# A GEGLU kernel's first weight chunk: its second pair of blocks by seven products in place of plain matmuls

## The chip, the cores and the metric

The kernel runs on one core of one Trainium2 chip. The metric is the device time of one execution in microseconds (us). One run of each kernel is profiled.

## The reference

```python
def reference(x, w_gate, w_up, w_down):      # x 1 x 2048 x 1024, w_gate and w_up 1024 x 3584, w_down 3584 x 1024, bf16
    return (_gelu(x @ w_gate) * (x @ w_up)) @ w_down
```

## The kernel before

The kernel takes the tokens in two halves of 1024 (h), each as two token blocks of 512 (tb). It takes the 3584 columns of the weights in chunks of 512, each of two **pairs** of 128-column blocks. A **plain unit** is one column block against one token block: 8 matmuls for gate, 8 for up, then a gelu on ScalarE and a multiply on VectorE. A pair against both token blocks is four plain units, 64 matmuls. Nearly every pair is instead done in the manner of Strassen and Winograd, as a 2 x 2 block product with **seven products** in place of eight: 56 matmuls. For that it needs sums of weight blocks (S1 to S4, per pair, mostly on GpSimd) and sums of blocks of x (T1 to T4, once per half, on VectorE), and M1 to M7 are combined in the PSUM banks by copies (ScalarE) and additions (VectorE). M1 and M2 use unsummed bf16 blocks; the other five use f32 sums (with f32 copies of one block each in M3 and M4).

Only the first chunk of the first half is plain, in all its eight units, because the sums are not there yet. All instructions of an engine run in program order; `dve`, `act`, `pool`, `pe` and `sp` fix that order.

```python
    for kd in range(KH, KD):
        load_xT(xT, 0, 0, kd, kd + 1)
        if kd == KH + 1:
            for j in range(2):
                load_w(first, j, 5, KD, act, 0, FA)
    for j in range(2):
        load_w(first, j, 0, KD, sp, FA, FG)
    for k0 in range(0, KD, KH):
        load_xT(xT, 0, 1, k0, k0 + KH)
    new_chunk((0, 1))
    for j in range(2):
        load_w((0, 1), j, 0, KD)

    # [cut: half()]

    def t_sum(name):
        def b(j, l):
            return xT[l][:, half(j), :]

        t0 = ("t1", "t2", "t3", "b22", "t4").index(name) * KH * TB
        t = t_mem[:, t0 : t0 + KH * TB].rearrange("p (a b) -> p a b", b=TB)
        tsum[name] = t
        sub = ALU.subtract
        tt = nc.vector.tensor_tensor
        if name == "t1":
            dve(tt(out=t, in0=b(0, 1), in1=b(0, 0), op=sub))
        elif name == "t2":
            t1 = tsum["t1"].bitcast(F32)
            dve(tt(out=t, in0=b(1, 1), in1=t1, op=sub))
        elif name == "t3":
            dve(tt(out=t, in0=b(1, 1), in1=b(0, 1), op=sub))
        elif name == "t4":
            t2 = tsum["t2"].bitcast(F32)
            dve(tt(out=t, in0=b(1, 0), in1=t2, op=sub))
        else:
            for c in range(KH):
                act(nc.scalar.copy(out=t[:, c, :], in_=b(1, 1)[:, c, :]))

    # [cut: gelu() is one ScalarE activation, mult() one VectorE multiply into hT, unit_out() both]

    def unit(hT, bset, fi, tb):
        for b, w_sb in zip(bset, chunks[first]):
            for kd in range(KD):
                mm_gu(banks[b], w_sb, fi, tb, kd)
        unit_out(hT, bset, fi, tb)

    # [cut: transpose_x0(), which transposes half of block 0 on TensorE]

    def first_units(hT):

        wg, wu = chunks[first]
        held = (VB, RB)
        transpose_x0(0)
        for kd, j in [(kd, j) for kd in range(KD) for j in range(2)]:
            for u in range(2):
                mm_gu(banks[held[u][j]], (wg, wu)[j], u, 0, kd)
            if (j, kd) == (1, 0):

                transpose_x0(1)
        for u in range(2):
            unit_out(hT, held[u], u, 0)

    # [cut: s_sum(h, pair, j, name): with a(i, kh) the weights of f-block i and contraction half kh,
    #  s1 = a(1,0) + a(1,1), s2 = s1 - a(0,0), s3 = a(0,0) - a(1,0), s4 = a(0,1) - s2; on GpSimd,
    #  or on VectorE if on_dve; a22 is a ScalarE copy of a(1,1)]
    # [cut: pair_quads() up to here; its mm() is the four matmuls of one half of a product, done() runs
    #  what is hung on a point, prep() makes the next pair's sums, add_m5() adds M5 on VectorE]

        def m2():
            for j in range(2):
                mm(P_[j], j, block(key, j, 0, 1), b21, False)
                if j == 0:
                    g[0] = gelu(banks[P_[0]], nxt is None)
                else:
                    mult(hT, g[0], banks[P_[1]], f0, 0)

        def do_m5(j):
            mm(V_[j], j, s(j, "s1"), tsum["t1"], True)
            m5[j] = m_pool.tile([P, TB], F32, name=f"m5_{j}")
            act(nc.scalar.copy(out=m5[j][:], in_=banks[V_[j]][:]))
            prep(j, "s1")

        def do_m6(j):
            mm(QB[j], j, s(j, "s2"), tsum["t2"], False)
            act(nc.scalar.copy(out=banks[RB[j]][:], in_=banks[QB[j]][:]))

        for j in range(2):
            mm(P_[j], j, block(key, j, 0, 0), b11, True)
            act(nc.scalar.copy(out=banks[QB[j]][:], in_=banks[P_[j]][:]))
        behind = len(pending) > 0
        if behind:

            pending.pop()()
        done("m2 of last")
        if behind:
            if nxt is None:
                m2()
                done("m2")
            else:
                pending.append(m2)
            order = (do_m6, 0), (do_m6, 1), (do_m5, 0), (do_m5, 1)
        else:
            pending.append(m2)
            order = (do_m5, 0), (do_m6, 0), (do_m6, 1), (do_m5, 1)
        for f, j in order:
            f(j)
            if (f, j) == (do_m6, 1):
                done("m6")
        for j in range(2):
            add_m5(QB[j], QB[j])
            prep(j, "s2")
        done("m5")
        for j in range(2):
            mm(RB[j], j, s(j, "s3"), tsum["t3"], False)
            add_m5(V_[j], RB[j])
            prep(j, "s3")
            if j == 0:
                g[1] = gelu(banks[V_[0]], nxt is None)
            else:
                mult(hT, g[1], banks[V_[1]], f0 + 1, 1)
        done("m7")
        for j in range(2):
            mm(QB[j], j, s(j, "s4"), tsum["b22"], False)
            prep(j, "s4")
            if j == 0:
                g[2] = gelu(banks[QB[0]], nxt is None)
            else:
                mult(hT, g[2], banks[QB[1]], f0, 1)
        done("m3")
        for j in range(2):
            mm(RB[j], j, s(j, "a22"), tsum["t4"], False)
            prep(j, "a22")
            if j == 0:
                g[3] = gelu(banks[RB[0]], nxt is None)
            else:
                mult(hT, g[3], banks[RB[1]], f0 + 1, 0)

    # [cut: the down projection]

        if h == 0:
            first_units(hT)
            unit(hT, PB, 2, 0)
            t_sum("t1")
            unit(hT, QB, 3, 0)
            t_sum("t2")
            t_sum("b22")
            unit(hT, VB, 0, 1)
            t_sum("t3")
            for name in S_NAMES:
                for j in range(2):
                    s_sum(0, PPG, j, name)
            unit(hT, RB, 1, 1)
            t_sum("t4")
            unit(hT, QB, 2, 1)
            unit(hT, VB, 3, 1)
            first_pair = PPG
```

Of the kernel before, what the change touches and what calls it, by code (L numbers as in the profile page):

```python
# [34 lines left out]
def kernel(  # L35
# [171 lines left out]
    for kd in range(KH, KD):  # L207
        load_xT(xT, 0, 0, kd, kd + 1)
        if kd == KH + 1:
            for j in range(2):  # L210
                load_w(first, j, 5, KD, act, 0, FA)
    for j in range(2):
        load_w(first, j, 0, KD, sp, FA, FG)
    for k0 in range(0, KD, KH):
        load_xT(xT, 0, 1, k0, k0 + KH)
    new_chunk((0, 1))
    for j in range(2):
        load_w((0, 1), j, 0, KD)
# [4 lines left out]
    def half(j):  # L223
        return slice(j * KH, (j + 1) * KH)

    def t_sum(name):
        def b(j, l):
            return xT[l][:, half(j), :]

        t0 = ("t1", "t2", "t3", "b22", "t4").index(name) * KH * TB  # L230
        t = t_mem[:, t0 : t0 + KH * TB].rearrange("p (a b) -> p a b", b=TB)
        tsum[name] = t
        sub = ALU.subtract
        tt = nc.vector.tensor_tensor
        if name == "t1":
            dve(tt(out=t, in0=b(0, 1), in1=b(0, 0), op=sub))
        elif name == "t2":
            t1 = tsum["t1"].bitcast(F32)
            dve(tt(out=t, in0=b(1, 1), in1=t1, op=sub))
        elif name == "t3":  # L240
            dve(tt(out=t, in0=b(1, 1), in1=b(0, 1), op=sub))
        elif name == "t4":
            t2 = tsum["t2"].bitcast(F32)
            dve(tt(out=t, in0=b(1, 0), in1=t2, op=sub))
        else:
            for c in range(KH):
                act(nc.scalar.copy(out=t[:, c, :], in_=b(1, 1)[:, c, :]))


    def mm_gu(ps, w_sb, fi, tb, kd):  # L250
# [33 lines left out]
    def unit_out(hT, bset, fi, tb):  # L284
        mult(hT, gelu(banks[bset[0]]), banks[bset[1]], fi, tb)

    def unit(hT, bset, fi, tb):
        for b, w_sb in zip(bset, chunks[first]):
            for kd in range(KD):
                mm_gu(banks[b], w_sb, fi, tb, kd)  # L290
        unit_out(hT, bset, fi, tb)

    def transpose_x0(q):

        parts = [(2 * q, 0, 4), (2 * q + 1, 0, 4)]
# [15 lines left out]
            else:  # L311
                act(nc.scalar.copy(out=xT[0][:, kd, cols], in_=tp[:, cols]))  # L312

    def first_units(hT):

        wg, wu = chunks[first]
        held = (VB, RB)
        transpose_x0(0)
        for kd, j in [(kd, j) for kd in range(KD) for j in range(2)]:
            for u in range(2):  # L320
                mm_gu(banks[held[u][j]], (wg, wu)[j], u, 0, kd)
            if (j, kd) == (1, 0):

                transpose_x0(1)
        for u in range(2):
            unit_out(hT, held[u], u, 0)


    ssum = {}
# [4 lines left out]
        w_sb = chunks[(key[0], key[2] // PPG)][j]  # L334
        return w_sb[:, half(kh), fi * P : (fi + 1) * P]

    def s_sum(h, pair, j, name, on_dve=False):
        key = (h, "p", pair)

        def a(i, kh):  # L340
            return block(key, j, i, kh)

        if on_dve and name in ("s1", "s2", "s3"):

            if j == 0:
                first_s[name] = wd_pool.tile([P, WDT, D], BF16, name="wd_sb")
            t = first_s[name][:, j, :].bitcast(F32R)
        else:
            s0 = (2 * S_NAMES.index(name) + j) * KH * P
            t = s_mem[:, s0 : s0 + KH * P]  # L350
        t = t.rearrange("p (a b) -> p a b", b=P)
        ssum[(h, pair, j, name)] = t

        def tt(in0, in1, op):
            if on_dve:
                dve(nc.vector.tensor_tensor(out=t, in0=in0, in1=in1, op=op))
            else:
                pool(nc.gpsimd.tensor_tensor(out=t, in0=in0, in1=in1, op=op))  # L358

        if name == "s1":  # L360
            tt(a(1, 0), a(1, 1), ALU.add)
        elif name == "s2":
            s1 = ssum[(h, pair, j, "s1")].bitcast(F32)
            tt(s1, a(0, 0), ALU.subtract)
        elif name == "s3":
            tt(a(0, 0), a(1, 0), ALU.subtract)
        elif name == "s4":
            s2 = ssum[(h, pair, j, "s2")].bitcast(F32)
            tt(a(0, 1), s2, ALU.subtract)
        else:  # L370
            act(nc.scalar.copy(out=t, in_=a(1, 1)))  # L371
# [6 lines left out]
    def pair_quads(hT, h, pair, nxt, then):  # L378
# [67 lines left out]
        if behind:  # L446
# [3 lines left out]
            else:  # L450
                pending.append(m2)
            order = (do_m6, 0), (do_m6, 1), (do_m5, 0), (do_m5, 1)
        else:
            pending.append(m2)
            order = (do_m5, 0), (do_m6, 0), (do_m6, 1), (do_m5, 1)
# [349 lines left out]
    for h in range(NH):  # L805
        hT = hT_pool.tile([P, KF, SH], BF16, name="hT")
        first_pair = 0
        if h == 0:
            first_units(hT)
            unit(hT, PB, 2, 0)  # L810
            t_sum("t1")
            unit(hT, QB, 3, 0)
            t_sum("t2")
            t_sum("b22")
            unit(hT, VB, 0, 1)
            t_sum("t3")
            for name in S_NAMES:
                for j in range(2):
                    s_sum(0, PPG, j, name)
            unit(hT, RB, 1, 1)  # L820
            t_sum("t4")
            unit(hT, QB, 2, 1)
            unit(hT, VB, 3, 1)
            first_pair = PPG
            xs = [(tb, kd) for tb in (1, 0) for kd in range(KD)]
            new_x(1)
            stage_load(0)
# [1 line left out]
        for pair in range(first_pair, NPAIR):  # L829
            then = {}  # L830
            if pair % PPG == 0 and (pair // PPG + 1) * PPG < NPAIR:
# [6 lines left out]

                if key not in chunks:
                    then["m2 of last"] = [load_chunk]  # L840
            if h == 0:

                n = [min(4 * (pair - first_pair + d), NSTEP) for d in range(3)]
                steps = [lambda k=k: stage_step(k) for k in range(n[0], n[1])]
                new = range((n[1] + 2) // 3, (n[2] + 2) // 3)

# [130 lines left out]
```

## Time and profile before

| | before |
|---|---|
| median of 4 runs | 541.58 us (541.51 to 543.56) |
| span of the profiled run | 539.7 us |
| TensorE busy | 535.1 us, 99% |
| VectorE's first multiply (block 0 of the first pair done) | 13.26 us |
| first product of the first seven-product pair | 33.80 us |
| last matmul's record ends, last ScalarE copy starts | 536.32, 536.41 us |

The engines' timelines: the columns are start, length, engine, line, operation, output and input, count, and in brackets how long the engine was idle before and what released it.

```profile
13.26 1.28 DVE L276 TENSOR_TENSOR hT<-w_mem,bank 128x512 bf16<-128x512 f32 x2 [6.30 <-PE bank L252]
...
33.80 1.89 PE L386 MATMUL bank<-xT,w_mem 128*128 128x512 bf16 x8
...
531.63 4.69 PE L656 MATMUL bank<-t_mem,s_mem 128*128 128x512 f32 x20
...
536.41 0.59 ACT L709 CAST o_sb<-bank 128x512 bf16<-128x512 f32 x1 [5.76 <-PE bank L656]
```

From the first multiply (13.26) to the third pair's first matmul (33.80) is the **stretch** that the change rewrites: 20.54 us. From the end of the last matmul to the start of the last ScalarE copy is the **tail**: 536.41 - 536.32 = 0.09 us.

### The profile page before, as it was taken

What the parts mean: (1) busy time and instruction counts of PE and PEld (TensorE: products, weight loads), DVE (VectorE), ACT (ScalarE), POOL (GpSimd) and SP (SyncE); (2) the same over time, 40 slices, a digit from 0 to 9 for tenths busy, and PEclk for the clock granted to TensorE, in tenths of its full rate; (3) what the DMA queues carried; (4) which work ended last, traced back from release to release, by engine and by line L of the source; (5) the groups of instructions that cost most, each with busy time, mean ns of one, the idle gap of its engine ahead of it and who ended that gap; (6) DMA issues with size and microseconds to landing.
All of it is one profiled execution on the core that took longest, in us unless ns stands there. A gap on an engine that the chain in (4) does not pass through costs nothing.

```text
span 539.7 us, 7102 instructions
## 1 busy us (share of the span) xinstructions
PE 535.1 (99%) x2392; PEld 374.5 (69%) x2392; DVE 354.9 (66%) x466; ACT 258.9 (48%) x438; POOL 235.0 (44%) x206
## 2 busy tenths in 40 slices
PE   9999999999999999999999999999999999999997
PEld 3457777666776676767776677777777766866865
DVE  1767777787775997889574434444444469969951
ACT  2435555555555319216465555555555551452270
POOL 0197777777776000000056776666777730000000
PEclk9999999999999999999999999999999999999999
DMA  9928577696827876779950405041331466677946
GB/s 233 310 82 230 185 242 237 184 286 195 277 76 252 299 244 227 249 265 313 327 182 1 155 2 156 7 149 57 99 106 51 157 204 213 226 241 246 291 145 207
DMA packets 84771, 102.70 MB, mean 190 GB/s; under 512 B 18688, under 2 KB 66304, under 8 KB 84736
## 3 DMA queue, kind: packets, MB, share of 16 engines
q1 hardware_dynamic: 61936, 80.30, 46.2%
q10 hardware_dynamic: 22800, 21.96, 13.2%
q8 instruction: 19, 0.31, 0.2%
q14 instruction: 16, 0.13, 0.1%
HBM read 85.98 MB, written 12.58 MB: 183 GB/s over the span
## 4 chain that ended last, share of the span: by engine, by line
PE 98%; DMA 1%; ACTq 0%; ACT 0%; issue 0%
PE bank L386 61%; PE bank L656 33%; PE bank L252 5%; DMA w_mem<-in_w_gate_dram 1%; ACTq L161 0%; ACT xT L312 0%; ACT o_sb L709 0%; ACTq L167 0%; ACTq L709 0%
## 5 line engine op out<-in xcount | busy, mean ns | idle before, releaser
L386 PE MATMUL bank<-t_mem,s_mem 128*128 128x512 f32 x1016 | 239.8, 394 | 0.0
L386 PEld LDWEIGHTS bank<-t_mem,s_mem 128*128 128x128 f32 x1016 | 190.8, 188 | 41.9
L358 POOL TENSOR_TENSOR s_mem<-w_mem 128x512 fp32r<-128x512 bf16 x100 | 115.8, 1178 | 201.3 <-DMA w_mem<-in_w_up_dram 104.6
L276 DVE TENSOR_TENSOR hT<-w_mem,bank 128x512 bf16<-128x512 f32 x104 | 71.3, 686 | 92.4 <-PE bank L386 46.3
L656 PE MATMUL bank<-t_mem,s_mem 128*128 128x512 f32 x544 | 127.2, 392 | 0.0
L656 PEld LDWEIGHTS bank<-t_mem,s_mem 128*128 128x128 f32 x544 | 102.1, 188 | 22.2 <-issue 0.2
L409 DVE TENSOR_TENSOR bank<-bank,m 128x512 f32<-128x512 f32 x104 | 67.3, 694 | 46.9 <-ACT m L431 45.3
L386 PE MATMUL bank<-xT,w_mem 128*128 128x512 bf16 x416 | 94.3, 380 | 0.0
L271 ACT ACTIVATE w_mem<-bank 128x512 f32<-128x512 f32 x104 | 61.9, 596 | 57.7 <-DVE bank L409 32.7
L386 PEld LDWEIGHTS <-w_mem 128*128 128x128 bf16 x416 | 38.7, 98 | 49.7 <-issue 6.5
L566 DVE TENSOR_TENSOR t_mem<-w_mem 128x1024 fp32r<-128x1024 bf16 x56 | 65.5, 1216 | 0.0
L358 POOL TENSOR_TENSOR s_mem<-w_mem,s_mem 128x512 fp32r<-128x512 bf16 x50 | 62.1, 1267 | 0.0
L358 POOL TENSOR_TENSOR s_mem<-s_mem,w_mem 128x512 fp32r<-128x512 f32 x50 | 59.6, 1212 | 0.0
L371 ACT CAST s_mem<-w_mem 128x512 fp32r<-128x512 bf16 x52 | 32.0, 616 | 33.1 <-PE bank L386 29.1
L436 ACT COPY bank<-bank 128x512 f32<-128x512 f32 x52 | 29.6, 570 | 38.1 <-PE bank L386 38.1
L631 DVE TENSOR_TENSOR s_mem<-hT 128x512 fp32r<-128x512 bf16 x52 | 34.2, 685 | 10.2 <-PE bank L656 9.5
L656 PEld LDWEIGHTS <-hT 128*128 128x128 bf16 x224 | 21.3, 98 | 26.6 <-issue 2.1
L431 ACT COPY m<-bank 128x512 f32<-128x512 f32 x52 | 30.5, 587 | 17.1 <-PE bank L386 17.1
L440 ACT COPY bank<-bank 128x512 f32<-128x512 f32 x52 | 29.6, 570 | 13.5 <-PE bank L386 13.5
L709 ACT CAST o_sb<-bank 128x512 bf16<-128x512 f32 x28 | 15.4, 585 | 39.6 <-PE bank L656 39.6
L591 DVE TENSOR_TENSOR o_sb<-wd_sb,o_sb 128x512 fp32r<-128x512 bf16 x28 | 29.4, 1051 | 0.5
L252 PE MATMUL bank<-xT,w_mem 128*128 128x512 bf16 x128 | 28.4, 379 | 0.3 <-DVE xT L310 0.2
(42 smaller groups left out, 250.4 us busy)
## 6 DMA issues: line engine op xcount, KB each, us to landing
t_mem<-t_dram SPq DMA_DIRECT2D x56, 512.0 KB, 5.3
w_mem<-in_w_gate_dram ACTq DMA_DIRECT2D x10, 1024.0 KB, 5.6
w_mem<-in_w_up_dram ACTq DMA_DIRECT2D x10, 1024.0 KB, 9.1
wd_sb<-in_w_down_dram SPq DMA_DIRECT2D x28, 256.0 KB, 5.0
t_dram<-o_sb SPq DMA_DIRECT2D x28, 256.0 KB, 2.4
wd_sb<-in_w_down_dram SPq DMA_DIRECT2D x12, 512.0 KB, 8.8
w_mem<-in_w_down_dram SPq DMA_DIRECT2D x10, 512.0 KB, 6.1
w_mem<-in_w_down_dram SPq DMA_DIRECT2D x4, 1024.0 KB, 6.3
```

Of the source, the lines that this page charges most:

```text
L252: nc.tensor.matmul(ps[:], lhsT=w_sb[:, kd, fi * P : (fi + 1) * P], rhs=xT[tb][:, kd, :], start=(kd == 0), stop=(kd == KD - 1),)
L271: act(nc.scalar.activation(out=g_sb, in_=ps[:], func=ACT.Gelu_apprx_tanh))
L276: nc.vector.tensor_tensor(out=hT[:, fc, tb * TB : (tb + 1) * TB], in0=g_sb, in1=ps[:], op=ALU.mult,)
L358: pool(nc.gpsimd.tensor_tensor(out=t, in0=in0, in1=in1, op=op))
L371: act(nc.scalar.copy(out=t, in_=a(1, 1)))
L386: nc.tensor.matmul(banks[bank][:], lhsT=lhs[:, c, :], rhs=rhs[:, c, :], start=start and c == 0, stop=c == KH - 1, skip_group_check=True,)
L409: nc.vector.tensor_tensor(out=banks[dst][:], in0=banks[src][:], in1=m5[j][:], op=ALU.add)
L431: act(nc.scalar.copy(out=m5[j][:], in_=banks[V_[j]][:]))
L436: act(nc.scalar.copy(out=banks[RB[j]][:], in_=banks[QB[j]][:]))
L566: dve(nc.vector.tensor_tensor(out=t, in0=in0, in1=in1, op=ALU.subtract))
L631: dve(nc.vector.tensor_tensor(out=t, in0=in0, in1=in1, op=op))
L656: nc.tensor.matmul(banks[bset[u]][:], lhsT=lhs(i, u), rhs=rhs(i), start=start and i == 0, stop=stop and i == NS - 1, skip_group_check=True,)
```

## The change

The first chunk's second pair is done by seven products as well. For this its sums must be ready some 14 us earlier than the first sums were before. So both token blocks of the first pair are done first, the transposes of x for block 1 go ahead of the second pair's weights in SyncE's queue (as 2 + 2 + 4 blocks instead of 4 + 4), T3 follows T1 and T2 at once on VectorE, S3 moves from GpSimd to VectorE, and M2, which needs no sums, stands right behind M1 to give the sums time.

```diff
@@ loads at the start
+    for k0, k1 in ((0, 2), (2, KH), (KH, KD)):
+        load_xT(xT, 0, 1, k0, k1)
     for j in range(2):
         load_w(first, j, 0, KD, sp, FA, FG)
-    for k0 in range(0, KD, KH):
-        load_xT(xT, 0, 1, k0, k0 + KH)
     new_chunk((0, 1))
... (t_sum takes a range of contraction blocks, so far always the whole one; unit() goes; part() runs the
    matmuls of units 0 and 1, or of one of them, over a range of contraction blocks)
-    def first_units(hT):
... (the same four held banks for units 0 and 1 of token block 0)
+    def first_pair_units(hT):
+        held = (VB, RB)
+        transpose_x0(0)
+        part(held, 0, 0, 1)
+        transpose_x0(1)
+        part(held, 0, 1, KD)
         for u in range(2):
             unit_out(hT, held[u], u, 0)
+        held = (QB, PB)
+        part(held, 1, 0, KH)
+        t_sum("t1")
+        t_sum("t2")
+        t_sum("b22")
+        t_sum("t3")
+        for u in range(2):
+            part(held, 1, KH, KD, (u,))
+            unit_out(hT, held[u], u, 1)
+        for j in range(2):
+            s_sum(0, 1, j, "s3", True, False)
+        for name in ("s1", "s2", "s4"):
+            for j in range(2):
+                s_sum(0, 1, j, name)
@@ pair_quads
             else:
                 pending.append(m2)
             order = (do_m6, 0), (do_m6, 1), (do_m5, 0), (do_m5, 1)
+        elif "m2" in then:
+            m2()
+            done("m2")
+            order = (do_m5, 0), (do_m5, 1), (do_m6, 0), (do_m6, 1)
         else:
@@ main loop
         if h == 0:
-            first_units(hT)
-            unit(hT, PB, 2, 0)
-            t_sum("t1")
... (the other units and sums of the first chunk)
-            first_pair = PPG
+            first_pair_units(hT)
+            first_pair = 1
...
-            if h == 0:
+            if h == 0 and pair < PPG:
+                then = {
+                    "m2": [lambda j=j: s_sum(0, pair, j, "a22") for j in range(2)]
+                    + [lambda: t_sum("t4")],
+                }
+            if h == 0 and pair >= PPG:
... (the staging of the down weights counts from pair PPG as before)
```

More of the change, by code (lines that the diff above doesn't have):

```diff
@@ L224, in half, with t_sum @@
         return slice(j * KH, (j + 1) * KH)
-    def t_sum(name):
+    def t_sum(name, c0=0, c1=KH):
         def b(j, l):
-            return xT[l][:, half(j), :]
+            return xT[l][:, j * KH + c0 : j * KH + c1, :]
         t0 = ("t1", "t2", "t3", "b22", "t4").index(name) * KH * TB
@@ L232, in t_sum @@
         tsum[name] = t
-        sub = ALU.subtract
-        tt = nc.vector.tensor_tensor
-        if name == "t1":
-            dve(tt(out=t, in0=b(0, 1), in1=b(0, 0), op=sub))
-        elif name == "t2":
-            t1 = tsum["t1"].bitcast(F32)
-            dve(tt(out=t, in0=b(1, 1), in1=t1, op=sub))
-        elif name == "t3":
-            dve(tt(out=t, in0=b(1, 1), in1=b(0, 1), op=sub))
-        elif name == "t4":
-            t2 = tsum["t2"].bitcast(F32)
-            dve(tt(out=t, in0=b(1, 0), in1=t2, op=sub))
-        else:
-            for c in range(KH):
-                act(nc.scalar.copy(out=t[:, c, :], in_=b(1, 1)[:, c, :]))
+        t = t[:, c0:c1, :]
+        if name == "b22":
+            for c in range(c1 - c0):
+                act(nc.scalar.copy(out=t[:, c, :], in_=b(1, 1)[:, c, :]))
+            return
+        in0, in1 = {
+            "t1": lambda: (b(0, 1), b(0, 0)),
+            "t2": lambda: (b(1, 1), tsum["t1"].bitcast(F32)[:, c0:c1, :]),
+            "t3": lambda: (b(1, 1), b(0, 1)),
+            "t4": lambda: (b(1, 0), tsum["t2"].bitcast(F32)[:, c0:c1, :]),
+        }[name]()
+        dve(nc.vector.tensor_tensor(out=t, in0=in0, in1=in1, op=ALU.subtract))
     def mm_gu(ps, w_sb, fi, tb, kd):
@@ L285, in unit_out @@
         mult(hT, gelu(banks[bset[0]]), banks[bset[1]], fi, tb)
-    def unit(hT, bset, fi, tb):
-        for b, w_sb in zip(bset, chunks[first]):
-            for kd in range(KD):
-                mm_gu(banks[b], w_sb, fi, tb, kd)
-        unit_out(hT, bset, fi, tb)
     def transpose_x0(q):
@@ L312, in transpose_x0, with part @@
                 act(nc.scalar.copy(out=xT[0][:, kd, cols], in_=tp[:, cols]))
-    def first_units(hT):
-        wg, wu = chunks[first]
+    def part(held, tb, k0, k1, us=(0, 1)):
+        for kd in range(k0, k1):
+            for j in range(2):
+                for u in us:
+                    mm_gu(banks[held[u][j]], chunks[first][j], u, tb, kd)
+    def first_pair_units(hT):
         held = (VB, RB)
         transpose_x0(0)
-        for kd, j in [(kd, j) for kd in range(KD) for j in range(2)]:
-            for u in range(2):
-                mm_gu(banks[held[u][j]], (wg, wu)[j], u, 0, kd)
-            if (j, kd) == (1, 0):
-                transpose_x0(1)
+        part(held, 0, 0, 1)
+        transpose_x0(1)
+        part(held, 0, 1, KD)
         for u in range(2):
             unit_out(hT, held[u], u, 0)
+        held = (QB, PB)
[10 more added lines that the diff above has]
+        for name in ("s1", "s2", "s4"):
+            for j in range(2):
+                s_sum(0, 1, j, name)
     ssum = {}
@@ L335, in block, with s_sum @@
         return w_sb[:, half(kh), fi * P : (fi + 1) * P]
-    def s_sum(h, pair, j, name, on_dve=False):
+    def s_sum(h, pair, j, name, on_dve=False, staged=True):
         key = (h, "p", pair)
@@ L341, in a @@
             return block(key, j, i, kh)
-        if on_dve and name in ("s1", "s2", "s3"):
+        if on_dve and staged and name in ("s1", "s2", "s3"):
             if j == 0:
@@ L808 @@
         if h == 0:
-            first_units(hT)
-            unit(hT, PB, 2, 0)
-            t_sum("t1")
-            unit(hT, QB, 3, 0)
-            t_sum("t2")
-            t_sum("b22")
-            unit(hT, VB, 0, 1)
-            t_sum("t3")
-            for name in S_NAMES:
-                for j in range(2):
-                    s_sum(0, PPG, j, name)
-            unit(hT, RB, 1, 1)
-            t_sum("t4")
-            unit(hT, QB, 2, 1)
-            unit(hT, VB, 3, 1)
-            first_pair = PPG
+            first_pair_units(hT)
+            first_pair = 1
             xs = [(tb, kd) for tb in (1, 0) for kd in range(KD)]
@@ L840 @@
                     then["m2 of last"] = [load_chunk]
-            if h == 0:
-                n = [min(4 * (pair - first_pair + d), NSTEP) for d in range(3)]
+            if h == 0 and pair < PPG:
[4 more added lines that the diff above has]
+            if h == 0 and pair >= PPG:
+                n = [min(4 * (pair - PPG + d), NSTEP) for d in range(3)]
                 steps = [lambda k=k: stage_step(k) for k in range(n[0], n[1])]
```

## The prediction

> **What bounds the kernel now.** I read the page's busy row first, then its chain that ended last, then the chain in order of time.
>
> ```profile
> PE 535.1 (99%) x2392; PEld 374.5 (69%) x2392; DVE 354.9 (66%) x466; ACT 258.9 (48%) x438; POOL 235.0 (44%) x206
> ...
> PE 98%; DMA 1%; ACTq 0%; ACT 0%; issue 0%
> ```
>
> ```profile
> 8.61 25.34 PE bank L252 x116
> 33.96 150.70 PE bank L386 x672
> 184.66 87.89 PE bank L656 x392
> ```
>
> The reader is to see that TensorE is the path from 8.6 us to the end, without a gap, and that no other engine is above 66%. L252 is the plain first chunk that this change attacks; L386 are the pairs done by seven products; L656 is the down projection, untouched. So only two things can move the time: fewer matmuls in the first chunk, and new gaps of TensorE there.
>
> The rates. ScalarE's timeline shows one gelu per plain unit of 16 bf16 matmuls, and the first copy (L440) of each seven-product pair:
>
> ```profile
> 15.00 0.60 ACT L271 ACTIVATE w_mem<-bank 128x512 f32<-128x512 f32 x1 [1.29 <-PE bank L252]
> ...
> 32.27 0.60 ACT L271 ACTIVATE w_mem<-bank 128x512 f32<-128x512 f32 x1 [2.86 <-PE bank L252]
> ```
>
> Between these two gelus lie five units: 17.27 / 5 = 3.454 us each, 215.9 ns per matmul. The 12 pairs of the second chain line take 150.70 / 12 = 12.56 us for 56 matmuls; 16 of them are bf16 (3.45 us), so the 40 in f32 take 9.10 us, 227.6 ns each. 128 plain matmuls at 215.9 ns are 27.63 us, and 5.24 us (first matmul in TensorE's timeline) plus that plus some 1 us of transposes gives the 33.8 us at which the first product starts: the first chunk has no hidden stall to win back.
>
> **What the Trainium skill says.** "TensorE: Matmul & The Clock Gate", section "Back-to-back issue gap", gives N / 2.4 + 2.5 ns when warm, 215.8 ns for N = 512; the trace has 215.9. "SBUF — State Buffer", section "Who interferes with whom", says that a VectorE instruction with two SBUF inputs contends with a GpSimd instruction that reads SBUF, and that the shared port is an exclusive lock. The trace agrees to a tenth of a microsecond (VectorE's and GpSimd's timelines):
>
> ```profile
> 24.31 2.28 DVE L241 TENSOR_TENSOR t_mem<-xT 128x2048 fp32r<-128x2048 bf16 x1
> 27.76 3.10 DVE L244 TENSOR_TENSOR t_mem<-xT,t_mem 128x2048 fp32r<-128x2048 bf16 x1
> ```
>
> ```profile
> 25.83 1.78 POOL L358 TENSOR_TENSOR s_mem<-w_mem 128x512 fp32r<-128x512 bf16 x1 [1.68 <-DMA w_mem<-in_w_up_dram]
> 27.57 4.32 POOL L358 TENSOR_TENSOR s_mem<-s_mem,w_mem 128x512 fp32r<-128x512 f32 x2
> ```
>
> GpSimd's sum at 25.83 finds the port held by T3 until about 26.45 and ends 1.16 us after that; T4 at 27.76 waits for GpSimd's operation of 27.57 to let go after some 1.0 us, runs its 2.28 us to 30.86, and GpSimd's next one ends 1.0 us later. Each waiter gets the port as the holder leaves; they alternate. "DMA: Bandwidth & Descriptors", section "Queues, rings and completion order", says that on each DMA engine a queue's descriptors are consumed in ring order; so what is issued first on SyncE's queue mostly lands first, which is the reason for moving the transposes of x.
>
> **The change part by part.**
>
> *Removed and added on TensorE.* Before, the four f-blocks of the first chunk are plain: 128 matmuls. After, blocks 0 and 1 are plain on both token blocks (64), and blocks 2 and 3 form a pair (56). One plain pair, 64 x 215.9 = 13.82 us, becomes 12.56 us: **1.26 us** less on the path that sets the end, 541.53 to 540.27 us if nothing waits. That is 0.23%, the whole possible gain.
>
> *The x transposes.* They now stand ahead of the two 512 KB weight loads in SyncE's queue. Before, those weights landed at 12.6 and 14.4 us, the two transposes at 16.4 and 18.3 us (issue plus time to landing in the DMA view). The same bytes in the new order end at the same 18.3 us, so I estimate the 2+2+4 blocks in at about 11.4, 12.5 and 14.6 us and the weights at about 16.5 (gate) and 18.3 (up). TensorE finishes token block 0 at 13.05 us, wants the second block's first transposes then, those of blocks 2-3 at 14.8, the rest at 16.5, and the second pair's weights (M1) at 13.05 + 32 x 0.2159 = 19.96 and 20.8. Each has one to three microseconds of room.
>
> *The sums.* They are the same kinds of work, but now due 14 us earlier. VectorE's order is fixed (the instruction order of both kernels shows it): two multiplies, T1, T2, T3, the multiplies of units 0 and 1, S3 twice, the multiply behind M2, T4, then the additions of M5. GpSimd has S1, S2, S4, two each. From the rows above: T 2.28 us, S on GpSimd 1.15, S on VectorE 0.68, multiply 0.69.
>
> - VectorE's multiplies end at 14.4; T1 to 16.6, T2 to 18.8. GpSimd, waiting since the gate weights landed, takes the port for 1.0 us; T3 runs 19.65 to 21.9.
> - Unit 0's multiply, done by gelu time at 19.1, is behind T3: 21.85 to 22.5. It frees the bank into which M1's second result is copied: copy to 23.15. M2's second half could start at 22.55 and starts at 23.2: **0.65 us lost**.
> - M5, M6, M7 then run without waiting: S1 is ready at 19.8 and 23.0 against 24.1 and 25.0; S2 at 24.1 and 25.65 against 25.9 and 26.8; S3 at 24.6 and 26.2 against 27.7.
> - S3, T4 and GpSimd's S2 and S4 alternate on the port, so T4 runs from 27.06 and ends at 29.3. The addition of M5 into M3's bank stands behind it and ends at 29.95. M3 could start at 23.2 + 0.86 + 24 x 0.2276 = 29.5, starts at 30.0: **0.5 us lost**.
> - Afterwards the third pair starts at 33.65 us against 33.8: its sums (GpSimd, from 29.2 on, eight of 1.15 us) are done before their products.
>
> Sum: -1.26 + 0.65 + 0.5 = -0.1 us: 541.4 us. This is the walk that I consider likeliest.
>
> **The rivals.**
>
> *A: one more GpSimd operation ahead of T3.* If the gate weights land before T2 starts (16.5), GpSimd takes the port both before T2 and before T3, and everything behind T3 moves by 1.0 us: 542.4 us. For it: my landing estimate is 16.5, on the edge. Against: more separate transposes make the queue later rather than earlier.
>
> *C: the port hardly bites.* If the gate weights land after T3 has started (18.8 or later), or VectorE keeps the port between back-to-back sums, the first loss falls to 0.0 to 0.2 us and the second to about 0.3 to 0.5: 540.3 to 540.9. For it: S3 and T3 were placed early on purpose, which looks tuned for this; and two-microsecond gaps were seen between issue and first bytes (the 1 MB load issued at 16.08 has its bytes only from 18.3). Against: the alternation in the lines above.
>
> *D: a transfer becomes the wait.* If the weights of the second pair land after 20 us, M1 waits for DMA, with up to 1 us. Against: the bytes ahead of them are the same as those that were in by 18.3 us before.
>
> *E: the gain appears in full or more* because VectorE or GpSimd work leaves the path elsewhere. Against: TensorE has no gap later, so nothing else can shorten.
>
> **Range and chances.** A 0.2 x 542.4, the walk 0.4 x 541.4, C 0.4 x 540.5 make 541.2 us. D belongs to the tail. The range runs from near the full saving, 540.4, to one port turn lost, 542.4. The three times of before spread from 541.51 to 543.56, so a single late run can hide the sign. Two per cent are 10.8 us; the moved stretch is 14 us long, and nothing in it can grow or shrink by that: same 0.98.
>
> **What would show it right or wrong.** The chain should read L249 x some 58 and then the products; M1 of the second pair should start near 20.0 us with no DMA wait before it. On VectorE, T3 should take 3.2 us (1.0 of them for the port) rather than 2.28; ScalarE's second copy behind M1 should wait for VectorE's multiply; the product bank's matmuls should show gaps of 0.65 us before M2's second half and of 0.5 before M3, with VectorE as releaser. Third pair's M1 at 33.6 us; from there the trace is a copy of the old one. It is wrong if T1, T2 and T3 take 2.28 us each while GpSimd works, if TensorE waits for xT of block 1, or if the third pair itself stalls on GpSimd's S sums, which start later than they did before.

## The result

The changed kernel's median was **541.85 us** (541.73 to 541.90, 4 runs), that of before 541.58. The ratio was 0.9994 with a 95% interval of 0.9976 to 1.0012: the same. The ratio is taken over the fast runs of the same rounds, so it is not quite the ratio of the medians; here the one high value of before, 543.56, pulls it under 1.

The page of the changed kernel, busy row and the chain by engine:

```profile
PE 534.0 (99%) x2384; PEld 377.4 (70%) x2384; DVE 361.8 (67%) x472; ACT 263.4 (49%) x446; POOL 245.6 (45%) x212
...
PE 94%; SPq 3%; DMA 2%; DVE 1%; issue 0%; ACT 0%; ACTq 0%
```

TensorE has 8 matmuls fewer, and in the chain other engines now hold 6% of the span. Where they do, the chain in order of time says:

```profile
15.78 8.49 DMA w_mem<-in_w_up_dram
...
24.33 1.65 DVE s_mem L363
25.98 0.60 DVE hT L273
26.58 2.58 DVE t_mem L244
29.16 0.62 DVE bank L416
29.78 0.14 issue
29.92 154.61 PE bank L393 x688
```

From 24.33 to 29.92 us the end is no longer set by TensorE but by VectorE's work: S3 (L363), a multiply (L273), T4 (L244) and the addition of M5 (L416), which releases M3 at 29.92 us. The DMA line above them, and with it the 5% for SyncE's queue (SPq) and DMA, is not a wait that the program has: the load issued at 15.78 is that of the next chunk and landed at 25.94 us, after this S3 had begun; the second pair's own up weights had landed at 19.48, and this S3 simply follows the other half's S3 on VectorE. From 29.92 on it is TensorE without a gap, as before. TensorE's timeline shows the same place from its own side:

```profile
19.48 2.76 PE L393 MATMUL bank<-xT,w_mem 128*128 128x512 bf16 x12
23.04 1.02 PE L393 MATMUL bank<-xT,w_mem 128*128 128x512 bf16 x4 [0.80 <-ACT bank L447]
23.71 5.91 PE L393 MATMUL bank<-t_mem,s_mem 128*128 128x512 f32 x24
29.92 3.89 PE L393 MATMUL bank<-t_mem,s_mem 128*128 128x512 f32 x16 [0.30 <-DVE bank L416]
33.65 1.90 PE L393 MATMUL bank<-xT,w_mem 128*128 128x512 bf16 x8
```

The first line is M1 and the first half of M2, the second line the second half of M2, then M5, M6 and M7 (24 matmuls), then M3 and M4 (16), then the third pair. Two waits stand in brackets, 0.80 and 0.30 us. Their **cost is larger than what is shown**, since a matmul's record (0.38 us) is longer than the distance to the next one (0.216 us), and the idle time is counted from the record's end. Twelve matmuls from 19.48 end at 22.07 by distance; the next starts at 23.04: 0.97 us lost. For the second wait: 23.04 plus 4 x 0.2159 plus 24 x 0.2276 is 29.37, and M3 starts at 29.92: 0.55 us lost.

Who made M2 wait is in the timelines of VectorE, ScalarE and GpSimd:

```profile
16.28 2.29 DVE L244 TENSOR_TENSOR t_mem<-xT,t_mem 128x2048 fp32r<-128x2048 bf16 x1
18.49 3.24 DVE L244 TENSOR_TENSOR t_mem<-xT 128x2048 fp32r<-128x2048 bf16 x1
21.65 1.27 DVE L273 TENSOR_TENSOR hT<-w_mem,bank 128x512 bf16<-128x512 f32 x2
...
22.41 0.57 ACT L447 COPY bank<-bank 128x512 f32<-128x512 f32 x1 [1.25 <-DVE hT L273]
...
17.84 4.91 POOL L365 TENSOR_TENSOR s_mem<-w_mem 128x512 fp32r<-128x512 bf16 x2 [16.53 <-DMA w_mem<-in_w_gate_dram]
```

T3 (second line) took 3.24 us where T1 and T2 (first line) took 2.29, because GpSimd had started on S1 and held the SBUF port they share. Unit 0's multiply, ready to run since its gelu ended at 18.3, stood behind T3 in VectorE's order until 21.65. It reads the PSUM bank into which ScalarE copies the second half of M1; so that copy waited 1.25 us, and M2 for the copy.

**The balance.** The stretch is 33.65 - 12.75 = 20.90 us, against 20.54 before, although 1.26 us of matmul work is gone: 20.54 - 1.26 = 19.28 is what it would be without waits, plus 0.97, plus 0.55, leaves 0.10. Nearly all of it lies in M3 and M4, which took 33.65 - 29.92 = 3.73 us where 16 x 0.2276 is 3.64: the second matmul after the wait followed only after 0.31 us. So the new stretch is **0.36 us longer** than the old one. The profiled run hides that, because it began better: its first multiply came at 12.75 us, 0.51 us earlier than before. And there is a loss that belongs to no sum, at the very end:

```profile
531.72 4.47 PE L667 MATMUL bank<-t_mem,s_mem 128*128 128x512 f32 x19
...
536.55 0.59 ACT L720 CAST o_sb<-bank 128x512 bf16<-128x512 f32 x1 [6.04 <-PE bank L667]
```

The last matmul's record ends at 536.19, 0.13 us earlier than before, but the last copy starts 0.36 us later instead of 0.09. Together: -0.51 (start) + 0.36 (stretch) + 0.27 (tail) = +0.12 us, and the spans differ by 0.2 (539.9 against 539.7).

### The profile page after: what moved, and what is told of

Read it like the earlier page. It is cut to its first block, busy times and chain, and to the rows that moved or that the text cites. A ratio compares the mean times of both kernels' runs of the same rounds, so it can differ in the third digit from the quotient of the medians.

```text
span 539.9 us, 7120 instructions
## 1 busy us (share of the span) xinstructions
PE 534.0 (99%) x2384; PEld 377.4 (70%) x2384; DVE 361.8 (67%) x472; ACT 263.4 (49%) x446; POOL 245.6 (45%) x212
## 4 chain that ended last, share of the span: by engine, by line
PE 94%; SPq 3%; DMA 2%; DVE 1%; issue 0%; ACT 0%; ACTq 0%
PE bank L393 61%; PE bank L667 33%; SPq L172 2%; DMA w_mem<-in_w_up_dram 2%; SPq L161 1%; DVE t_mem L244 0%; DVE s_mem L363 0%; DVE bank L416 0%; DVE hT L273 0%; ACT o_sb L720 0%; SPq L167 0%; ACTq L720 0%
## 5 line engine op out<-in xcount | busy, mean ns | idle before, releaser
L393 PE MATMUL bank<-t_mem,s_mem 128*128 128x512 f32 x1056 | 249.6, 394 | 0.3 <-DVE bank L416 0.3
L393 PEld LDWEIGHTS bank<-t_mem,s_mem 128*128 128x128 f32 x1056 | 198.2, 188 | 44.3 <-issue 0.7
L365 POOL TENSOR_TENSOR s_mem<-w_mem 128x512 fp32r<-128x512 bf16 x102 | 120.3, 1200 | 190.6 <-DVE t_mem L244 102.8
L273 DVE TENSOR_TENSOR hT<-w_mem,bank 128x512 bf16<-128x512 f32 x104 | 71.2, 687 | 87.0 <-PE bank L393 46.6
L667 PE MATMUL bank<-t_mem,s_mem 128*128 128x512 f32 x544 | 127.2, 392 | 0.0
L667 PEld LDWEIGHTS bank<-t_mem,s_mem 128*128 128x128 f32 x544 | 102.1, 188 | 22.1
L416 DVE TENSOR_TENSOR bank<-bank,m 128x512 f32<-128x512 f32 x108 | 69.8, 694 | 45.2 <-ACT m L438 44.1
L393 PE MATMUL bank<-xT,w_mem 128*128 128x512 bf16 x432 | 98.1, 380 | 0.8 <-ACT bank L447 0.8
L393 PEld LDWEIGHTS <-w_mem 128*128 128x128 bf16 x432 | 40.2, 98 | 52.6 <-issue 7.9
L365 POOL TENSOR_TENSOR s_mem<-w_mem,s_mem 128x512 fp32r<-128x512 bf16 x52 | 67.3, 1315 | 0.0
L443 ACT COPY bank<-bank 128x512 f32<-128x512 f32 x54 | 30.8, 570 | 38.8 <-PE bank L393 38.8
L438 ACT COPY m<-bank 128x512 f32<-128x512 f32 x54 | 31.8, 589 | 17.9 <-PE bank L393 17.9
L447 ACT COPY bank<-bank 128x512 f32<-128x512 f32 x54 | 30.8, 570 | 13.4 <-PE bank L393 12.2
L574 ACT CAST t_mem<-w_mem 128x1024 fp32r<-128x1024 bf16 x28 | 26.9, 1048 | 0.0
```

Of the source, the lines that this page charges most:

```text
L273: nc.vector.tensor_tensor(out=hT[:, fc, tb * TB : (tb + 1) * TB], in0=g_sb, in1=ps[:], op=ALU.mult,)
L365: pool(nc.gpsimd.tensor_tensor(out=t, in0=in0, in1=in1, op=op))
L393: nc.tensor.matmul(banks[bank][:], lhsT=lhs[:, c, :], rhs=rhs[:, c, :], start=start and c == 0, stop=c == KH - 1, skip_group_check=True,)
L416: nc.vector.tensor_tensor(out=banks[dst][:], in0=banks[src][:], in1=m5[j][:], op=ALU.add)
L667: nc.tensor.matmul(banks[bset[u]][:], lhsT=lhs(i, u), rhs=rhs(i), start=start and i == 0, stop=stop and i == NS - 1, skip_group_check=True,)
```

## The experiments

Theory: the saving is real, but the sums of the second pair are due at once with TensorE's own work, T1 to T4 and S1 to S4 share one SBUF port between VectorE and GpSimd, and VectorE's fixed order hands the delay on to TensorE, at M2 and at M3. Rivals: the x or weight transfers are the wait; the port does not matter, only the order does; TensorE has no loss in the stretch, and the 0.3 us of the result is luck of the start.

Times of single runs jump by microseconds (the kernel before, run in the same jobs, had 541.12 to 545.79), and part of that is the start: VectorE's first multiply came between 12.75 and 14.34 us in the fourteen profiles. The change of the loads does not show in it: it came at 13.01 to 13.44 us in the four with the old order of loads (before, e3, e5, e10), 13.26 on average, and at 13.29 on average in the ten with the new one. The stretch and the tail do not contain the start, and the times are given beside them. All kernels gave correct results.

| run | stretch, us | tail, us | median, us | before in the same job | ratio (95%) |
|---|---|---|---|---|---|
| before | 20.54 | 0.09 | 541.58 | | |
| changed | 20.90 | 0.36 | 541.85 | 541.58 | 0.9994 (0.9976 to 1.0012) |
| c1, changed again | 20.91 | 0.36 | 542.86 | 542.29 | 1.0015 (0.9982 to 1.0049) |
| e1, GpSimd behind T3 | 23.71 | 0.36 | 544.64 | 542.88 | 1.0029 (1.0011 to 1.0047) |
| e2, multiply ahead of T3 | 20.35 | 0.38 | 542.03 | 542.88 | 0.9986 (0.9968 to 1.0003) |
| e3, x behind the weights | 24.07 | 0.08 | 545.36 | 542.20 | 1.0056 (1.0037 to 1.0076) |
| e4, B22 in one copy | 20.90 | 0.08 | 542.93 | 542.88 | 1.0002 (0.9984 to 1.0020) |
| e5, before with 8 copies more | 20.54 | 0.08 | 541.95 | 542.88 | 0.9990 (0.9969 to 1.0010) |
| e6, S3 on GpSimd | 21.68 | 0.37 | 543.08 | 542.20 | 1.0014 (0.9995 to 1.0034) |
| e7, e2 and T4 in halves | 20.10 | 0.36 | 542.09 | 542.20 | 0.9992 (0.9975 to 1.0009) |
| e8, e7 and e4 | 20.10 | 0.09 | 541.29 | 542.20 | 0.9989 (0.9968 to 1.0010) |
| c2, e8 again | 20.08 | 0.09 | 541.68 | 542.29 | 0.9985 (0.9958 to 1.0012) |
| e9, M2 later | 20.90 + 1.73 | 0.36 | 544.39 | 542.29 | 1.0039 (1.0000 to 1.0077) |
| e10, before with 14 copies more | 20.54 | 0.08 | 541.43 (one run) | 542.29 | |

The stretch repeats to 0.02 us between jobs (changed and c1, e8 and c2, before and e5 and e10), where the times repeat to about 1 us.

### e1: GpSimd's S sums wait for T3

```diff
         t_sum("t3")
+        pool_behind_dve()
```

> Changed kernel with one wait more: GpSimd's first S sum waits for T3, so that T1, T2 and T3 never meet it at the shared port. Port theory (the same SBUF port serves both, one instruction at a time): T3 takes 2.29 us instead of 3.24, unit 0's multiply ends about 1 us earlier, and the 0.80 us gap of TensorE before M2's second half shrinks to under 0.1 us. But the port is then idle of GpSimd's work from 17.8 to 20.7 us and S1, S2, S4 end 2 to 3 us later, so gaps of 1 to 2 us open before M6 and M7, and the third pair starts at about 34.9 us instead of 33.65: some 1.2 us slower, near 543.1 us. Rival (the loss is only VectorE's order, the port does not matter): T3 still 2.3 or 3.2 us, no later gaps, time equal or lower than 541.85.

VectorE's timeline, and GpSimd's first line:

```profile
18.76 2.29 DVE L244 TENSOR_TENSOR t_mem<-xT 128x2048 fp32r<-128x2048 bf16 x1
...
21.13 2.73 POOL L366 TENSOR_TENSOR s_mem<-w_mem 128x512 fp32r<-128x512 bf16 x2 [19.82 <-DVE t_mem L244]
```

T3 is back at 2.29 us, and the wait before M2's second half is gone (0.22 us of distance at the most). So the port is what lengthened T3. But GpSimd, which started at 21.13 instead of 17.84 us, is now late itself; TensorE's waits, 12 to 38 us (in total, how often, the longest):

```profile
PE bank L394 <- POOL s_mem L366: 2.2, 2, 2.0
```

That is S2, for both halves of M6. The stretch grew to 23.71 us. I had expected about 1.2 us of loss against the changed kernel and it was 2.8. The table of windows shows the rest (length, then the busy time of TensorE, its weight loads, VectorE, ScalarE and GpSimd with counts, TensorE's granted clock, the DMA engines' share and GB/s):

```profile
24.00:28.60 4.60, 2.42 (x10) 1.34 (x8) 4.19 (x4) 1.92 (x4) 4.60 (x3) 1.00 0.61 221
28.65:32.16 3.51, 3.51 (x9) 2.80 (x9) 0.70 (x1) 0.57 (x1) 3.51 (x4) 0.51 0.00 0
32.20:36.00 3.80, 3.80 (x18) 3.13 (x17) 2.78 (x4) 1.20 (x2) 3.80 (x4) 1.00 0.00 0
```

After the break TensorE ran at 0.51 of its clock for 3.5 us, 0.43 us from matmul to matmul, which cost about 1.6 us more than the waits. "TensorE: Matmul & The Clock Gate", section "What's actually happening", describes this: TensorE runs at half clock by default, and activity releases the throttle.

### e2: unit 0's multiply ahead of T3

```diff
-        t_sum("t3")
         for u in range(2):
             part(held, 1, KH, KD, (u,))
             unit_out(hT, held[u], u, 1)
+            if u == 0:
+                t_sum("t3")
```

> Changed kernel with unit 0's multiply ahead of T3 on VectorE, everything else the same. Theory: the multiply no longer waits for T3, the copy of M1's second half follows M1 at once, the 0.80 us gap before M2's second half is gone; T3's wait for the port (about 1 us) is partly hidden under the multiply; the gap before M3 (0.30 us) stays or grows to 0.3 to 0.8, because T4 and the addition behind it still end only some 0.4 to 0.6 us earlier. Third pair at 33.1 to 33.3 us instead of 33.65, time 0.4 to 0.5 us lower, 541.3 to 541.5. Rival (the bank of M1's second half is held by something else than that multiply, for example the gelu or a semaphore of M1): gap of 0.8 us stays, time as changed.

VectorE's timeline of e2 around T3, its start 1.59 us later than in the changed kernel (first multiply at 14.34):

```profile
20.07 0.68 DVE L273 TENSOR_TENSOR hT<-w_mem,bank 128x512 bf16<-128x512 f32 x1
20.66 2.65 DVE L244 TENSOR_TENSOR t_mem<-xT 128x2048 fp32r<-128x2048 bf16 x1
```

T3 still met the port (2.65 us), now without anybody waiting for it. The 0.97 us before M2's second half is gone, and the stretch is 0.55 us shorter, at the upper edge of what was expected (0.35 to 0.55). The other 0.42 came back: the waits that the trace gives for the weight loads of these products are now GpSimd's, at M6's second half (S2) and at M3 (S4):

```profile
PEld bank L394 <- POOL s_mem L366: 1.4, 3, 0.6
```

So the loss before M2 was the order on VectorE, and behind it stands the port.

### e3: the x transposes behind the weights again

```diff
-    for k0, k1 in ((0, 2), (2, KH), (KH, KD)):
-        load_xT(xT, 0, 1, k0, k1)
     for j in range(2):
         load_w(first, j, 0, KD, sp, FA, FG)
+    for k0 in range(0, KD, KH):
+        load_xT(xT, 0, 1, k0, k0 + KH)
```

> Changed kernel with one part undone: the transposes of block 1 of x again behind the two 512 KB weight loads and as two of four blocks. Theory: they land at 16.4 and 18.3 us as before the change, TensorE, which wants them at about 12.5, idles some 3.5 to 4 us for xT; the weights land at 12.6 and 14.4, so GpSimd's S sums are done before T2 and T3 want the port, the waits before M2's second half and M3 shrink (T3 under 2.4 us), and the loss is 2.5 to 3.5 us net: stretch 23.4 to 24.4 us. Rival (the order does not matter, transposes were early enough): stretch 20.9, no wait for xT.

TensorE's waits of e3:

```profile
PE bank L249 <- DMA xT<-in_x_dram: 2.9, 1, 2.9
```

and after this wait the clock was again 0.51 for 3.4 us (16.4 to 19.8 us). The waits before M2's second half and M3 were gone: TensorE came to M1 only at 24.78 us, when T3 was ending, and GpSimd had started on S1 at 12.39 us. T2 and T3 each met the port all the same (3.13 and 3.25 us; I had expected under 2.4), but nothing waited for them. The stretch of 24.07 us lies where it was expected, but partly by luck: the wait cost 3.26 - 0.22 = 3.04 us, less than the 3.5 to 4 expected, and the half clock, which I had not expected, 1.7 more (nine distances from 16.19 us took 3.63 us instead of 1.94); less the 1.52 us of the two waits that went, this is 3.2, and 3.17 was measured. The new order of the loads was therefore needed; it is not where the gain went.

### e6: S3 on GpSimd again

```diff
-        for j in range(2):
-            s_sum(0, 1, j, "s3", True, False)
-        for name in ("s1", "s2", "s4"):
+        for name in ("s1", "s2", "s3", "s4"):
```

> Changed kernel with one part undone: S3 of the second pair on GpSimd again, between S2 and S4. Theory: GpSimd has two more operations of 1.15 us before S4, VectorE two of 0.6 us fewer; T3 still meets the port, so the wait before M2's second half stays at about 0.97 us of pitch; S4 comes about 1 to 2 us later, M3 or M7 waits for GpSimd, stretch 21.5 to 22.2 us against 20.90. Rival (GpSimd has time to spare): stretch 20.6 to 20.9.

The stretch was 21.68 us, 0.78 longer, as the theory said; TensorE's waits:

```profile
PE bank L391 <- ACT bank L445: 0.8, 1, 0.8
PE bank L391 <- POOL s_mem L363: 0.5, 1, 0.5
```

The wait for ScalarE's copy before M2 is the same 0.8; a new one, for GpSimd's S3, stands before M7. Moving S3 to VectorE was worth 0.8 us.

### e9: M2 not right behind M1

```diff
-                    "m2": [lambda j=j: s_sum(0, pair, j, "a22") for j in range(2)]
+                    "m2 of last": [lambda j=j: s_sum(0, pair, j, "a22") for j in range(2)]
```

> Changed kernel with one part undone: the second pair's M2 waits, as for every other pair, until the next pair, so M5 follows M1. Theory (M2 behind M1 gives the sums 1.73 us of TensorE time to become ready): M5 is then due at 21.2 us, M6 at 22.1; S1 for the second half ends at 22.8 and S2 at about 24 and 25.4 us, so TensorE waits about 1.5 us more before M5 and M6; part of it comes back, as the loss before M3 falls. Stretch 21.5 to 22.8 us against 20.90, counted to the third pair's first matmul plus 1.73 us for the M2 that comes later. Rival (the place of M2 does not matter, T4 sets the end): 20.9.

The third pair's first matmul started 20.90 us after the first multiply, with M2's 1.73 us still to come: 22.63. TensorE's waits:

```profile
PE bank L393 <- POOL s_mem L365: 2.0, 2, 1.6
PE bank L393 <- DVE bank L416: 0.5, 1, 0.5
```

Both of GpSimd's waits are for S2, before the two halves of M6; that of gate stands behind S1 of up in GpSimd's order. M5 of gate had its S1. The edit also changes more than the place of M2: with M2 put off, the program takes the order M5, M6, M6, M5 (the last branch of `order`) in place of M5, M5, M6, M6, and T4 no longer has the multiply behind M2 in front of it. So the loss of 22.63 - 20.90 = 1.73 us is that of this form as a whole. The longest break from start to start was 2.01 us, and the clock stayed at 1.00 after it.

### e4, e5 and e10: the tail

e4 makes one ScalarE copy of the four of B22 (in both halves); e5 and e10 add 8 and 14 one-element ScalarE copies to the kernel before, at about 11 us.

```diff
-            for c in range(c1 - c0):
-                act(nc.scalar.copy(out=t[:, c, :], in_=b(1, 1)[:, c, :]))
+            act(nc.scalar.copy(out=t, in_=b(1, 1)))
```

> Changed kernel with the four ScalarE copies of B22 as one of four times the size, in both halves: 6 ScalarE instructions fewer, same work. It tests the tail. In the changed kernel the last ScalarE copy starts 0.36 us after the last matmul instead of 0.09, with no wait that the trace names, and one packet of the instruction queue lies in the last 4 us, which the kernel before does not have. Fetch theory (the last ScalarE instructions fall behind a boundary of instruction fetching): with 6 instructions fewer the packet and the slip of 0.27 us go, the time falls by about 0.3 us to 541.55. Rival (the slip is a semaphore or buffer wait that follows from the changed kernel's DMA lanes): the slip stays, the time stays at 541.85.

> Kernel before with 8 one-element ScalarE copies added at 11 us, where ScalarE idles: its ScalarE instruction count becomes that of the changed kernel. Fetch theory of the tail: the last ScalarE copy slips by about 0.27 us, an instruction packet lies in the last 4 us, time 541.8 to 541.9 against 541.55. Rival (the slip comes from DMA lanes or semaphores): no slip, time as before.

> Kernel before with 14 one-element ScalarE copies at 11 us: with the waits that are instructions of their own, ScalarE's stream is then 745 long as in the changed kernel, e1 and e2 (slip of 0.28 us at the last copy), where before has 731, e4 and e5 739 (no slip). Length theory: the last copy starts 0.36 us after its matmul instead of 0.09. Rival (the slip belongs to something else in the changed kernel): 0.09.

The end of e4 and then of e5, the last copy of each:

```profile
537.06 0.59 ACT L719 CAST o_sb<-bank 128x512 bf16<-128x512 f32 x1 [5.76 <-PE bank L666]
```

```profile
536.57 0.59 ACT L712 CAST o_sb<-bank 128x512 bf16<-128x512 f32 x1 [5.76 <-PE bank L659]
```

In e4 the slip is gone, with the stretch unchanged at 20.90. That fits a dependence on where the last copy stands in ScalarE's instruction stream, but e5 (as many ScalarE instructions on the page as the changed kernel, 446) shows no slip. I then counted the instruction stream with one more instruction for each further semaphore of an instruction that waits for several: before 731, e4 and e5 739, the changed kernel, e1 and e2 745. e10 brings the kernel before to 745 by this count and has no slip. **So its cause is open.** The chain in order of time narrows it. The end of before, and then of the changed kernel:

```profile
536.34 0.03 ACTq L709
536.37 0.04 issue
...
536.21 0.03 ACTq L720
536.23 0.32 issue
```

ScalarE's wait for the last matmul ends as promptly in both; the slip lies between this wait and the copy, where the profile shows nothing that ScalarE waits for ("issue"). So a late matmul, or a late signal from it, is not the cause. Fetching is not shown: the instruction packet that I had pointed to lies after the start of the last copy in the changed kernel, and one lies at the end of e4 and e5 too. But e10 does not refute it. In the traces the last packet of the instruction queue q14 starts 0.64 to 0.66 us after the start of the last copy in all seven kernels with the slip; in the others it starts 0.96 us after it (e3), 3.8 to 4.7 us after it (e4, e5, e8, c2), 11.3 us ahead of it (e10) or 23.7 us ahead of it (before). And counted by all records that the trace has of ScalarE, semaphore waits included, the seven with the slip have 708, e3 707, e5 705, e4, e8 and c2 701, before 697, but e10 711. So by this count e10 overshot the changed kernel. The kernel before, padded to exactly 708, was not run. What is shown is that the slip of 0.27 us is in every kernel with the changed loads and four copies of B22 (the changed one, c1, e1, e2, e6, e7, e9) and in none of the others.

### e7, e8 and the controls: a version with less loss

e7 is e2 with T4 in two halves, the second behind the two additions that M3 waits for; e8 is e7 with e4's single copy.

```diff
-                    + [lambda: t_sum("t4")],
+                    + [lambda: t_sum("t4", 0, 2)],
+                    "m5": [lambda: t_sum("t4", 2, KH)],
```

> Changed kernel with unit 0's multiply ahead of T3 (as in e2) and T4 as two halves on VectorE: the first where T4 stood, the second behind the two additions of M5 that M3 waits for. Compared by the stretch that leaves out the start: from VectorE's first multiply to TensorE's first matmul of the third pair, 20.54 us before, 20.90 changed, 20.35 in e2. Theory (M3 waits for GpSimd's S4 and for VectorE's additions because T4 holds the port and VectorE for 2.65 us): the half takes 1.2 to 1.7 us, S4 and the additions come about 1 us earlier, the wait before M3 falls from 0.42 us of pitch to under 0.15; M4 may wait 0.1 to 0.3 for the second half. Stretch 19.8 to 20.1, time 0.3 us under e2. Rival (the port's total work sets the end, the order does not matter): stretch as e2, 20.3 to 20.4, with the wait moved to M4.

> e7 and the B22 copies as one instruction (as in e4), which took the slip of 0.28 us at the tail away. Expected the best of all: stretch 19.8 to 20.1 us, last ScalarE copy within 0.1 us of its matmul, some 0.5 to 0.7 us under the kernel before and about 1.1 us under the changed kernel in the same rounds. If e7's order does nothing: stretch 20.35, 0.2 us under before.

> The changed kernel once more, unaltered, beside the best version on one chip: a control for the spread of the start (VectorE's first multiply began between 12.75 and 14.34 us in eight profiles of kernels that are alike up to there). Theory: the stretch from that multiply to the third pair's first matmul is 20.90 us again within 0.05, the last ScalarE copy starts 0.36 us after its matmul again; the time is about 0.6 us above the kernel before (0.36 in the stretch, 0.28 at the tail) apart from the luck of the start. Rival (changed equals before, and the first result's 0.3 us was the luck of the start): stretch 20.5.

> The version of e8 once more. Theory: stretch 20.10 us within 0.05, no slip at the tail, time about 0.4 us under before and 1.1 us under the changed kernel of the same rounds, less than the interval of five rounds may resolve. Rival (e8 was lucky): median at or above that of before.

e8's waits of the weight loads, 12 to 34 us:

```profile
PEld bank L393 <- DVE bank L416: 0.5, 1, 0.5
PEld bank L393 <- POOL s_mem L365: 0.5, 1, 0.5
```

M3 waits for nothing any more. What is left are two breaks of 0.25 us of distance each, and 0.11 more behind each for a late second matmul: M6's second half for S2 (GpSimd), M4 for the addition behind T4's second half (VectorE). The stretch is 20.10 us in e7 and e8 and 20.08 in c2, within or on the edge of what was expected, 0.8 us under the changed kernel and 0.44 to 0.46 under before, and the tail of e8 and c2 is that of before. Their medians lie 0.9 and 0.6 us under before's in their jobs, but both intervals include 1, so the **gain in time is not resolved** by these rounds; only the shorter stretch is shown. c1 repeated the changed kernel: stretch 20.91, tail 0.36, so the 0.36 us of the result is no luck of one run, and the rival that it equals before falls, as far as stretch and tail go; c1's time alone (1.0015, 0.9982 to 1.0049) would not show it. Untested is what the second pair's weights would do if they landed earlier with x still in front: they set when GpSimd comes to the port (17.84 us).

## Why the prediction was right or wrong

The range held (541.85 in 540.4 to 542.4) and the reason for it, that the saving is eaten at two named places, is what the trace shows. The point, 541.2, was 0.65 us too low, and the sign of the small change was wrong: measured without the start, the changed kernel is 0.36 + 0.27 = 0.63 us slower, where the walk had -0.1.

- *1.26 us fewer on TensorE.* Right: the balance of the stretch closes to 0.10 us with it.
- *The transfers.* The x transposes were put at 11.4, 12.5 and 14.6 us and landed at 11.24, 12.63 and 14.86 us. The weights were put at 16.5 and 18.3 and landed at 17.8 and 19.5, all in the order of issue: late by 1.2 us, without harm to M1, which was due at 19.48. e3 shows that the order mattered. Rival D did not occur.
- *T3 meets GpSimd once at the port.* Right: 3.24 us against "3.2". Rival A (twice) and rival C (hardly) did not occur; e1 shows that it is the port.
- *"0.65 us lost" before M2's second half.* **The term that was mis-sized**: 0.97 us. The chain was right, link by link (T3, unit 0's multiply, copy, M2). But from the end of block 0's matmuls to the end of T3 I had counted 21.9 - 13.05 = 8.85 us and it was 21.73 - 12.57 = 9.16: T1 starts 1.39 us after that end, not 1.35; T2 comes 2.32 us after T1, not 2.2; and T3 takes 3.24 us, where the walk has 18.8 to 21.9 = 3.1. Also, I asked for a visible gap of 0.65, and the visible gap understates the cost by 0.17.
- *"0.5 us lost" before M3.* Right: 0.55, by T4 and the addition behind it, as named. The chain in order of time shows both.
- *Third pair at 33.65 us.* Right to the hundredth, but by luck: the start was 0.51 us earlier than in the run before, and the stretch as much longer than in the walk, 20.90 against 33.65 - 13.26 = 20.39 (0.32 at M2, 0.05 at M3, 0.10 in small distances, the rest in the walk's rounding).
- *"From there the trace is a copy of the old one."* Wrong at the end: the tail of 0.27 us had no step in the prediction.
- *The signs.* The chain was to read L249 x some 58 and then the products. It has no L249 at all, because it runs over VectorE's sums up to 29.92 us. And the wait before M2's second half was to have VectorE as releaser; the trace names ScalarE's copy, with VectorE's multiply one link behind it.
- *Rival E's argument, that nothing else can shorten*, held.

## What to carry to other kernels

Work saved on the bounding engine at the start of a kernel can be paid back by the work that prepares it, if this has no time to spare there: here eight fewer matmuls needed eight sums and four more at once, on one shared port. When an engine's order is fixed, put the operation that another engine waits for ahead of the long one that is due later (e2: 0.55 us), and cut a long one where something short waits behind it (e7: another 0.25). Where a change is smaller than the run-to-run spread, compare a stretch between two marks inside the traces rather than the times: it repeated to 0.02 us where the medians moved by 1.

## What the Trainium skill lacked or had wrong

- "TensorE: Matmul & The Clock Gate", "What's actually happening": it puts the return to half clock after an idle window of about 3.4 us. In e1 the clock fell to 0.51 after a break of 2.36 us from start to start (with one of 0.66 us shortly before), in e3 after one of 3.26 us, and stayed there 3.5 and 3.4 us; after 2.01 us in e9 it stayed at 1.00. So a break well under the stated window can be enough.
- "TensorE: Matmul & The Clock Gate", "Back-to-back issue gap": its formula for a warm clock is right for bf16 (215.9 ns measured), but the page calls that the gap of an isolated matmul and puts a stream of them with N = 512 at some 131 ns; here the streams themselves took 215.9 ns. It has no figure for the f32 matmuls of this kernel, 227.6 ns. Nor does it price a break beyond the wait: after one the second f32 matmul follows after 0.31 to 0.34 instead of 0.23 us.
- "SBUF — State Buffer", "Who interferes with whom": right that VectorE's two-input sums and GpSimd's exclude each other (T3 3.24 us against 2.29, GpSimd's S1 held until T3 let go). It lacks how the port goes over when both keep asking: in the timelines here they alternate, operation by operation.
- No page has the spread of a kernel's start: the first multiply came between 12.75 and 14.34 us in fourteen profiles. The latest, e2, has a break of 1.12 us in block 0 for which the trace names a weight load; for the others the cause was not looked for.
- No page has the slip of 0.27 us of the last ScalarE copy, or a price for such a one. These runs did not settle its cause.
